# Attention with scores in 64-row tiles: the product with the remainder keys as two column tiles, and a rewritten table of steps

## The chip, the cores and the metric

The kernel runs on one core of one Trainium2 chip. The metric is the device time of one execution in microseconds (us), as the median of several runs. The engines of the core appear in the profile under short names: PE is the matrix engine (TensorE), PEld its weight loads, DVE the vector engine, ACT the scalar engine, POOL is GpSimd, and SP the engine whose queue issues most of the transfers (SPq).

## What is computed

Eight batches of eight heads of attention over 576 positions with head size 64, with an additive position bias, and after it a mixture of eight experts over the 4608 rows that attention gives.

```python
scores = scale * np.matmul(q, k.transpose(0, 1, 3, 2)) + bias
attn = np.exp(scores - scores.max(-1)); attn /= attn.sum(-1)
x = np.matmul(attn, v)                 # (8, 8, 576, 64), then rows of 512
...
e_idx = np.argmax(x @ w_gate + modality_bias[modality_id], axis=1)
for e in range(E):
    h = np.maximum(x[mask] @ w1[e], 0.0)
    out[mask] = gate_w[mask, None] * (h @ w2[e])
```

## The kernel before, in words

Three stages follow each other: the bias table (up to about 65 us), attention (to about 642 us) and the expert tiles (to the end). Attention works on pairs of heads: 8 batches times 4 pairs are 32 pairs, and the two heads of a pair lie on partitions 0 to 63 and 64 to 127.

576 positions are 512 and a remainder of 64. The 512 main positions are cut into four chunks of 128 queries, and the 64 remainder queries of both heads make a fifth chunk of 128 rows. For one pair and one chunk the score product (`scores`, L435) is twelve matmuls for chunks 0 to 3: each head contracts over its own 64 rows, so the two heads sit in two 64-row tiles of the array and go side by side. The fifth chunk is six matmuls over all 128 rows.

DVE reads the scores out of PSUM, adds the bias and takes the minimum (L449), ACT takes the exponential (L464), PE turns the result round in 128x128 blocks (`etrans`, L479 to L490), and DVE or ACT copy those out to `eT`, which holds the weights for the 512 main keys. POOL gathers the weights for the 64 remainder keys of both heads (`compact`, L469), PE turns these too (`rtrans`, L507), and ACT copies them to `rT`: 64 remainder keys of head 0 on partitions 0 to 63, those of head 1 below.

The product with the values (`av`) makes 576 query columns in two halves of 288. A half is eight matmuls with `eT` (L527), each with 128 rows of keys and 64 columns of one head. The two heads lie at columns 0 and 64 of the array (`tile_position=(0, 64 * h)`). To a half belongs one product with the remainder keys, `rem` (L521): `vrem` holds the remainder values of head 0 and 1 as a block diagonal with zeros beside, so one 128x128 matmul serves both heads. It opens half 0 and closes half 1. A matmul in f32 stands as two instructions in the trace (the transposes, and the score product with its f32r operands, stand as one).

The outer loop (`attention`) runs over n, the pair, and u = 0 to 4, the chunk. In step (n, u) it goes through the letters of `ORDER[u]`, and each engine gets its instructions in that order:

- `S` scores of chunk u, `f` and `e` exponentials of head 1 and head 0, `C` the remainder copy on POOL
- `t` and `T` transposes of the chunk that was scored two units earlier, heads 0 and 1 (for the fifth chunk, `T` is the small product L490)
- `R` the remainder transposes of pair n-1
- `a A b c` the value product of pair n-1: half 0 in two parts, half 1 in two parts
- `0 1 2` transposes of q, k and the remainder rows of pair n+1 (`prep`, L403 to L409). DVE copies them out as a high and a low part (L338 or L340, and L334)
- `L` and `V` issue loads of q and k for pair n+2, and of v for pair n+1; `q` and `k` are POOL's copies of q and k for pair n+2
- `X` and `B` take the next routing step of the batch finished before: `X` those with PE work (L779, L802, L850, L872), `B` those without

A digit after a letter puts the copies out of PSUM off by that many letters. Two banks of PSUM (`xps`) serve `R`, `0`, `1`, `2`, `X` and the value product in turn: whoever takes a bank waits for the copy out of the one that had it before. The last value products (pair 31) run in a step n = 32 without scores.

Of the kernel before, what the change touches and what calls it, by code (L numbers as in the profile page):

```python
# [22 lines left out]
S = 576  # L23
# [87 lines left out]
class Attn:  # L111
# [398 lines left out]
    def av(self, n, half, part):  # L510

        nc = self.nc
        if half == 0 and part == 0:
            self.xT[n] = self.xTb[n // NP % 2][:, n % NP, :]
        if part == 0:
            self.avps = self.xbank()
        v = self.vmain[n]
        sl = slice(HS * half, HS * half + HS)
        ps = self.avps[:, 0:HS]

        rem = lambda **kw: nc.tensor.matmul(ps, self.vrem[n % 2], self.rT[:, sl], skip_group_check=True, **kw)  # L521
        if half == 0 and part == 0:
            rem(start=True, stop=False)
        for k in (0, 1) if part == 0 else (2, 3):
            for h in range(2):
                o = slice(64 * h, 64 * h + 64)
                nc.tensor.matmul(  # L527
                    ps[o, :],
                    v[:, h, k, :],
                    self.eT[:, h, k, sl],  # L530
                    start=half == 1 and k == 0,
                    stop=half == 0 and k == 3,
                    tile_position=(0, 64 * h),
                    skip_group_check=True,
                )
        if part == 1:
            if half == 1:
                rem(start=False, stop=True)
            self.take(f"av{half}", self.xT[n][:, sl], ps)
            self.avps = None  # L540
            if half == 1:
                del self.vmain[n]

    def first_steps(self, route):
# [34 lines left out]


    ORDER = (
# [5 lines left out]
    )  # L587

    def attention(self):
# [889 lines left out]
```

## Time and profile before

| | |
|---|---|
| median of 3 runs | 1091.09 us (1089.97 to 1091.13) |
| the profiled execution | 1091.33 us, its span 1089.4 us |
| PE busy | 1066.4 us, 98% of the span |
| PEld, DVE, ACT, POOL busy | 842.9, 736.7, 678.8, 246.6 us |
| granted TensorE clock, mean | 0.999 |

The span reaches from the first to the last instruction; the profiled execution has 1.9 us around it. Busy is the time in which an engine had an instruction under way. Matmuls are pipelined and overlap in the record, so what a group of them costs PE is read from the start of the group to the start of the next one.

### The profile page before, as it was taken

What the parts mean: (1) busy time and instruction counts of PE and PEld (TensorE: products, weight loads), DVE (VectorE), ACT (ScalarE), POOL (GpSimd) and SP (SyncE); (2) the same over time, 40 slices, a digit from 0 to 9 for tenths busy, and PEclk for the clock granted to TensorE, in tenths of its full rate; (3) what the DMA queues carried; (4) which work ended last, traced back from release to release, by engine and by line L of the source; (5) the groups of instructions that cost most, each with busy time, mean ns of one, the idle gap of its engine ahead of it and who ended that gap; (6) DMA issues with size and microseconds to landing.
All of it is one profiled execution on the core that took longest, in us unless ns stands there. A gap on an engine that the chain in (4) does not pass through costs nothing.

```text
span 1089.4 us, 23080 instructions
## 1 busy us (share of the span) xinstructions
PE 1066.4 (98%) x8580; PEld 842.9 (77%) x8580; DVE 736.7 (68%) x1580; ACT 678.8 (62%) x1333; POOL 246.6 (23%) x521
## 2 busy tenths in 40 slices
PE   6989999999999999999999999999999999999997
PEld 3456777777777777777776779999999999898986
DVE  7987768677686776766868756587455665545544
ACT  6776766767667667676676765654455554444544
POOL 1012222414224224142242221331110001101110
PEclk9999999999999999999999999999999999999999
DMA  5983412212212122222221511112113621151500
GB/s 164 219 192 116 144 43 77 69 56 74 69 52 92 54 67 69 55 84 60 56 88 49 201 45 40 59 64 70 58 49 117 240 100 52 38 215 48 195 31 32
DMA packets 71960, 98.19 MB, mean 90 GB/s; under 512 B 23054, under 2 KB 47886, under 8 KB 71842
## 3 DMA queue, kind: packets, MB, share of 16 engines
q1 hardware_dynamic: 65826, 77.62, 24.0%
q0 software_dynamic: 5920, 19.03, 4.8%
q8 instruction: 69, 1.13, 0.4%
q14 instruction: 49, 0.40, 0.1%
q10 hardware_dynamic: 96, 0.00, 0.0%
HBM read 135.62 MB, written 23.90 MB: 146 GB/s over the span
## 4 chain that ended last, share of the span: by engine, by line
PE 90%; DVE 1%; issue 1%; ACT 1%; POOL 0%; POOLq 0%; DVEq 0%; ACTq 0%
PE p L1200 18%; PE p L1217 18%; PE sps L435 14%; PE xps L527 13%; PE eps L479 10%; PE xps L521 4%; PE xps L403 3%; PE xps L872 2%; PE xps L1180 2%; PE xps L507 1%; PE eps L485 1%; PE xps L779 1%; PE xps L409 1%; DVE Eb L449 1%; PE p L1399 1%
## 5 line engine op out<-in xcount | busy, mean ns | idle before, releaser
L464 ACT ACTIVATE Eb<-Eb,mn 128x576 f32<-128x576 f32 x288 | 221.1, 770 | 37.2 <-DVE mn L449 36.8
L449 DVE CUSTOM_DVE_ANT_0 Eb<-sps,NBm 128x576 f32<-128x576 f32 x256 | 183.7, 755 | 83.2 <-PE sps L435 70.3
L435 PE MATMUL sps<-QK 64*128 64x288 f32 (+1 forms) x1728 | 172.8, 311 | 3.1 <-DVE mn L449 2.0
L435 PEld LDWEIGHTS sps<-QK 64*128 64x128 f32 (+1 forms) x1728 | 133.4, 185 | 44.3 <-DVE QK L338 16.4
L1200 PE MATMUL p<-QK,w1hi 128*128 128x256 f32 x1136 | 160.9, 284 | 0.0
L1203 DVE SCALAR_TENSOR_TENSOR hl<-p,hh 128x512 fp32r<-128x512 f32 x72 | 49.7, 691 | 154.5 <-ACT hh L1202 154.5
L527 PE MATMUL xps<-eT,vraw 128*64 128x288 f32 x1024 | 151.8, 418 | 0.0
L1200 PEld LDWEIGHTS p<-QK,w1hi 128*128 128x128 f32 x1136 | 147.0, 192 | 2.9 <-issue 1.8
L479 PE MATMUL eps<-idf,Eb 128*128 128x128 f32 x1024 | 143.9, 276 | 0.0
L479 PEld LDWEIGHTS eps<-idf,Eb 128*128 128x128 f32 x1024 | 115.6, 141 | 12.7 <-issue 5.7
L336 ACT ACTIVATE eT<-eps 128x512 f32<-128x512 f32 x192 | 106.6, 590 | 28.8 <-PE eps L479 15.2
L1202 ACT ACTIVATE hh<-p 128x512 fp32r<-128x512 f32 x72 | 43.0, 598 | 116.6 <-PE p L1200 112.6
L1217 PE MATMUL p<-w2hi,hh 128*128 128x512 f32 x288 | 114.2, 396 | 0.0
L1217 PE MATMUL p<-w2hi,hl 128*128 128x512 f32 x288 | 112.5, 391 | 0.0
L1226 POOL DMA_INDIRECT out<-mo,idt x36 | 38.5, 1069 | 322.4 <-ACT QK L1183 222.2
L469 POOL COPY rem<-Eb 128x128 f32<-128x128 f32 x128 | 37.8, 296 | 301.8 <-ACT Eb L464 226.4
L527 PEld LDWEIGHTS xps<-eT,vraw 128*64 128x64 f32 x1024 | 62.2, 136 | 53.5 <-issue 25.4
L1163 DVE TENSOR_TENSOR w2lo<-NBm,w2hi 128x1024 fp32r<-128x1024 f32 x72 | 88.2, 1225 | 16.2 <-ACT w2hi L1162 16.1
L1200 PE MATMUL p<-QK,w1lo 128*128 128x256 f32 x568 | 91.3, 283 | 0.0
L1163 DVE TENSOR_TENSOR w1lo<-NBm,w1hi 128x1024 fp32r<-128x1024 f32 x72 | 84.2, 1231 | 0.2 <-ACT w1hi L1162 0.2
L1225 ACT ACTIVATE mo<-p,gates 128x512 f32<-128x512 f32 x36 | 24.8, 689 | 89.1 <-PE p L1217 74.4
L1200 PEld LDWEIGHTS p<-QK,w1lo 128*128 128x128 f32 x568 | 78.3, 192 | 0.0
(221 smaller groups left out, 1685.7 us busy)
## 6 DMA issues: line engine op xcount, KB each, us to landing
NBm<-moe_w SPq DMA_DIRECT2D x23, 2048.0 KB
NBm<-moe_w SPq DMA_DIRECT2D x44, 1024.0 KB
NBr<-xg SPq DMA_DIRECT2D x20, 516.0 KB
NBm<-xTb SPq DMA_DIRECT2D x32, 288.0 KB
qraw<-q SPq DMA_DIRECT2D x32, 256.0 KB
kraw<-k SPq DMA_DIRECT2D x32, 256.0 KB
vraw<-v SPq DMA_DIRECT2D x32, 256.0 KB
xg<-blank SPq DMA_DIRECT2D x9, 516.0 KB
```

Source lines behind the costliest of these rows:

```text
L336: self.nc.scalar.activation(out, ps, AF.Copy, scale=scale)
L435: nc.tensor.matmul(self.sps[h][:, half, 0:HS], QK[o, q, qs], QK[o, k, HS * half : HS * half + HS], start=i == 0, stop=i == 2, skip_group_c ...
L449: nc.vector.tensor_tensor_reduce(out=e.rearrange("p (t w) -> p t w", t=2), in0=self.sps[h][:, :, 0:HS], in1=nb.rearrange("p (t w) -> p t w ...
L464: self.nc.scalar.activation(e, e, AF.Exp, bias=mn, scale=-1.0, accum_out=sm)
L479: nc.tensor.transpose(ps[:, k, :], e[:, part, P * k : P * k + P], self.idf)
L521: rem = lambda **kw: nc.tensor.matmul(ps, self.vrem[n % 2], self.rT[:, sl], skip_group_check=True, **kw)
L527: nc.tensor.matmul(ps[o, :], v[:, h, k, :], self.eT[:, h, k, sl], start=half == 1 and k == 0, stop=half == 0 and k == 3, tile_position=(0, ...
L1163: self.nc.vector.tensor_tensor(l, w, h.bitcast(F32), op=ALU.subtract)
L1200: nc.tensor.matmul(ps[:, a, :], w[:, c, fs], x[:, c, :], start=i == 0, stop=i == len(ops) - 1)
L1202: nc.scalar.activation(hh[:, sl, :], ps, AF.Relu)
L1203: nc.vector.scalar_tensor_tensor(hl[:, sl, :], ps, 0.0, hh[:, sl, :].bitcast(F32), op0=ALU.max, op1=ALU.subtract)
L1217: nc.tensor.matmul(ps, h[:, f, sl], m[:, f, :], start=i == 0, stop=i == len(ops) - 1)
```

## The change

The remainder product becomes two matmuls of 64 columns, one for each head, at the same column positions as the products with `eT`. Each still contracts over all 128 rows of `rT` and takes 64 columns of `vrem`. The same edit rewrites `ORDER`.

```diff
-        rem = lambda **kw: nc.tensor.matmul(ps, self.vrem[n % 2], self.rT[:, sl], skip_group_check=True, **kw)
+        def rem(**kw):
+            for h in range(2):
+                o = slice(64 * h, 64 * h + 64)
+                nc.tensor.matmul(
+                    ps[o, :], self.vrem[n % 2][:, o], self.rT[:, sl], tile_position=(0, 64 * h), skip_group_check=True, **kw
+                )
+
...
     ORDER = (
-        "S X B t R1 T3 f e C L",
-        "01 t3 S a T 11 A f e C",
-        "S B t2 X e f k C q T2",
-        "b S e c B t1 T2 f V C",
-        "S B X 2 t T e B",
+        "L X S t R1 T3 f e C",
+        "0 t1 S f 11 e C a A2 B T",
+        "S B t3 e X f T3 C b",
+        "S c e k f t3 q T1 C",
+        "B S B X 22 t e V T1 B",
     )
```

What the table does to PE's instructions shows in unit u = 1 (here of a step in the middle of attention, from the last score matmul of chunk 1 to the first of chunk 2). The names are those of the code; xps_77 and xps_78 are the two PSUM banks. Before:

```order
L435 MATMUL sps_724<-QK_73 128x288
L521 MATMUL xps_77<-rT,vrem_110 128x288
L527 MATMUL xps_77<-eT,vraw_4133 64x288 x4
L490 MATMUL eps_726<-idf,Eb 64x64 x2
L403 MATMUL xps_78<-idf,qks_109 128x128 x4
L527 MATMUL xps_77<-eT,vraw_4133 64x288 x4
L435 MATMUL sps_723<-QK_73 128x288
```

and with the change (its lines are numbered 6 higher from `av` on):

```order
L435 MATMUL sps_724<-QK_73 128x288
L403 MATMUL xps_77<-idf,qks_109 128x128 x4
L524 MATMUL xps_78<-rT,vrem_110 64x288 x2
L533 MATMUL xps_78<-eT,vraw_4192 64x288 x8
L490 MATMUL eps_726<-idf,Eb 64x64 x2
L435 MATMUL sps_723<-QK_73 128x288
```

The transposes of k (L403) have moved ahead of the value product, whose two parts now stand in one piece behind the remainder product. The value product has moved to the other bank, xps_78, which the transposes of q used in the same unit.

On DVE the rows around the same place change in one step of four. The rows of before run from the second score read-out of chunk 0 (L449; its row without a source is the minimum that it leaves) to the first of chunk 1, in a step in which a routing step `B` (the one-hot rows, L827 to L837) falls on unit 0:

```order
L449 ISA Eb,mn_0_1_4619<-sps_724,NBm 128x576
L449 ISA mn_0_1_4619 128x1
L827 SCALAR_TENSOR_TENSOR oh<-lgs_4583,rev 128x40
L830 TENSOR_REDUCE mx_4601<-oh 128x5
L831 TENSOR_TENSOR oh<-oh,mx_4601 128x40
L832 TENSOR_TENSOR oh<-oh,valid 128x40
L837 TENSOR_TENSOR ohb<-ohb,oh 128x8 x5
L340 TENSOR_SCALAR QK_73<-xps_78 128x512
L334 SCALAR_TENSOR_TENSOR QK_73<-xps_78,QK_73 128x512
L449 ISA Eb,mn_1_0_4680<-sps_723,NBm 128x576
```

With the change:

```order
L449 ISA Eb,mn_0_1_4661<-sps_724,NBm 128x576
L449 ISA mn_0_1_4661 128x1
L340 TENSOR_SCALAR QK_73<-xps_78 128x512
L334 SCALAR_TENSOR_TENSOR QK_73<-xps_78,QK_73 128x512
L449 ISA Eb,mn_1_0_4704<-sps_723,NBm 128x576
L449 ISA mn_1_0_4704 128x1
L449 ISA Eb,mn_1_1_4706<-sps_724,NBm 128x576
L449 ISA mn_1_1_4706 128x1
L338 CAST QK_73<-xps_77 128x512
L334 SCALAR_TENSOR_TENSOR QK_73<-xps_77,QK_73 128x512
L833 SCALAR_TENSOR_TENSOR oh<-lgs_4613,rev 128x40
```

The nine one-hot instructions now come behind the copies of both q (L340, L334) and k (L338, L334). Elsewhere on DVE only small routing steps change places with a score read-out or a copy of `eT`. On PE the routing transposes of unit 0 (`X`) now come ahead of the scores of chunk 0, not behind them. On ACT the two copies of unit 1 that end half 0 (`rT`, 64 columns, and `xTb`) come behind the exponentials of chunk 1, and the copy that ends half 1 comes ahead of those of chunk 3. On SP the loads `L` move from the end of unit 0 to its start and `V` from unit 3 to unit 4; on POOL `k` and `q` move from unit 2 to unit 3.

## Rows read from the trace of the kernel before

**Rows 1.** The page: busy time of the engines; the group of the score read-outs

```profile
PE 1066.4 (98%) x8580; PEld 842.9 (77%) x8580; DVE 736.7 (68%) x1580; ACT 678.8 (62%) x1333; POOL 246.6 (23%) x521
...
L449 DVE CUSTOM_DVE_ANT_0 Eb<-sps,NBm 128x576 f32<-128x576 f32 x256 | 183.7, 755 | 83.2 <-PE sps L435 70.3
```

**Rows 2.** Busy time by stretch, attention's: us, each engine's busy, clock, DMA share

```profile
85.00:640.00 555.00, 552.37 (x4751) 404.97 (x4751) 399.65 (x1055) 387.20 (x924) 169.72 (x360) 1.00 0.26 79
```

**Rows 3.** What PE waited for from 85 to 640 us: total, times, longest

```profile
PE xps L507 <- DVE QK L1184: 1.6, 1, 1.6
PE sps L435 <- DVE QK L338: 0.5, 1, 0.5
```

**Rows 4.** Timeline of PE over unit 1 of a step: start, duration, instruction

```profile
312.23 0.60 PE L485 MATMUL eps<-idf,Eb 128*128 128x128 f32 x4
312.76 1.06 PE L435 MATMUL sps<-QK 64*128 64x288 f32 x12
313.75 0.75 PE L521 MATMUL xps<-rT,vrem 128*128 128x288 f32 x2
314.44 1.19 PE L527 MATMUL xps<-eT,vraw 128*64 128x288 f32 x8
315.46 0.28 PE L490 MATMUL eps<-idf,Eb 128*64 128x64 f32 x4
315.67 0.65 PE L403 MATMUL xps<-idf,qks 128*128 128x128 f32 x4
316.26 1.19 PE L527 MATMUL xps<-eT,vraw 128*64 128x288 f32 x8
317.38 0.80 PE L435 MATMUL sps<-QK 64*128 64x288 f32 x8
```

**Rows 5.** The same timeline, where half 1 ends in unit 3

```profile
305.14 0.75 PE L521 MATMUL xps<-rT,vrem 128*128 128x288 f32 x2
305.73 1.04 PE L479 MATMUL eps<-idf,Eb 128*128 128x128 f32 x8
```

**Rows 6.** Timeline of PE in the step without scores, n = 32

```profile
638.51 3.08 PE L527 MATMUL xps<-eT,vraw 128*64 128x288 f32 x24
641.52 0.75 PE L521 MATMUL xps<-rT,vrem 128*128 128x288 f32 x2
642.21 1.61 PE L779 MATMUL xps<-xTb,wgb 128*32 128x512 f32 x8
```

**Rows 7.** Timeline of PE: transposes behind a score group, and behind transposes

```profile
308.94 1.56 PE L435 MATMUL sps<-QK 64*128 64x288 f32 x12
310.43 0.66 PE L479 MATMUL eps<-idf,Eb 128*128 128x128 f32 x4
310.92 0.60 PE L507 MATMUL xps<-idf,rem 128*128 128x128 f32 x4
311.36 0.60 PE L479 MATMUL eps<-idf,Eb 128*128 128x128 f32 x4
```

**Rows 8.** Timeline of DVE, an ordinary step, and of PE behind it

```profile
349.21 0.69 DVE L334 SCALAR_TENSOR_TENSOR QK<-xps,QK 128x512 fp32r<-128x512 f32 x1
...
349.74 0.75 PE L521 MATMUL xps<-rT,vrem 128*128 128x288 f32 x2
```

**Rows 9.** Timeline of DVE in the step of rows 4, with one-hot

```profile
312.00 0.20 DVE L827 SCALAR_TENSOR_TENSOR oh<-lgs,rev 128x40 f32<-128x40 f32 x1
...
313.82 0.68 DVE L340 TENSOR_SCALAR QK<-xps 128x512 fp32r<-128x512 f32 x1
314.54 0.69 DVE L334 SCALAR_TENSOR_TENSOR QK<-xps,QK 128x512 fp32r<-128x512 f32 x1
```

**Rows 10.** What SP's queue waited for at the load of v

```profile
SPq L375 <- PE xps L527: 333.5, 30, 12.7
```

**Rows 11.** By line: weight loads in ns, least, median, most

```profile
L521 PEld LDWEIGHTS xps<-rT,vrem x128: 186/189/192, 83.0 to 641.6; 128*128 128x128 f32 x128
...
L527 PEld LDWEIGHTS xps<-eT,vraw x1024: 132/137/138, 83.7 to 640.9; 128*64 128x64 f32 x171
```

## The prediction

> **What bounds the kernel now.** I read the page's busy times first: PE is busy for 98% of the span, DVE for 68% and ACT for 62% [rows 1]. Then the stretch of attention alone: of 555 us PE is busy for 552, DVE for 400, ACT for 387, and the granted clock is 1.00 [rows 2], the higher of its two levels. PE's waits in this stretch come to about 2 us [rows 3]. So PE sets the pace here, and a busy PE is no proof that each of its slots is needed: matmuls overlap in the record. That is why I go on to the timeline and read slots, from the start of one group to the start of the next. They repeat to a few hundredths of a microsecond from step to step, so one step is enough.
>
> **What a slot is made of.** The clean measure is the long run of products with `eT` in the last step: 24 instructions from 638.51 to 641.52, 3.01 us [rows 6]. A group of eight takes 1.02 when the next group has the same column tiles (314.44 to 315.46) and 1.12 when it has not (316.26 to 317.38) [rows 4]; so leaving the tiling costs 0.10. (3.01 - 0.10) / 12 = 0.2425 us is what two instructions, one for each head, take side by side. Four of these are 0.97, so entering the tiling costs 1.02 - 0.97 = 0.05. Four transposes take 0.44 behind transposes (310.92 to 311.36) and 0.49 behind scores (310.43 to 310.92) [rows 7], and 0.53 when scores follow (312.23 to 312.76) [rows 4]: changing to or from them costs about 0.05 and 0.09 as well. The trace calls none of this waiting; it is time in which nothing new starts at a change of tile shape.
>
> The remainder product of before has a shape of its own among column tiles. In half 0 it holds PE from 313.75 to 314.44, 0.69 us [rows 4]; in half 1 from 305.14 to 305.73, 0.59 [rows 5]. As two column tiles it would be four instructions, two beside two: 2 x 0.2425 = 0.485. No row shows two column tiles that stream the same rows, so this has bounds: 0.485 if the two go side by side as the heads of L527 do, 0.97 if one goes after the other. I take 0.485, since form, row count and order of issue are those of L527.
>
> **Unit 1, half 0.** Before, from the end of the scores to the next scores: 0.69 remainder, 1.02 products, 0.21 the small product L490, 0.59 transposes of k, 1.12 products, in all 317.38 - 313.75 = 3.63 us [rows 4]. After: transposes of k between two other shapes, again 0.59; then remainder and all products in one piece, 0.05 + 10 x 0.2425 = 2.475; then L490, 0.21, which now pays for the change to scores in place of that to transposes. Sum 3.275. Saved: 0.355, of which 0.69 - 0.485 = 0.205 is the tiles, and 1.12 - 0.97 = 0.15 the order, since the products' second part is no longer entered and left on its own.
>
> **Unit 3, half 1.** The products before the remainder no longer leave their tiling; the remainder does it for them. The products' 1.12 [rows 4] and the remainder's 0.59 [rows 5] become 0.05 + 6 x 0.2425 + 0.10 = 1.605, 0.105 less. The eight transposes behind now pay 0.05 for a change that they did not have [rows 7]. Saved: 0.055.
>
> **The sum.** Steps n = 1 to 30 have both the value product and the transposes of k: 30 x (0.355 + 0.055) = 12.30 us. Step 31 has no transposes of k, so the tiles alone: 0.205 + 0.055 = 0.26. In step 32 transposes precede the first remainder product, which has their shape; it and the products take 0.485 + 0.10 + 1.02 before and 0.09 + 0.05 + 6 x 0.2425 after, 0.01 less, and the second falls from 0.69 [rows 6] to 0.485: together 0.215. In all 12.8 us. The profiled execution took 1091.33 us; less 12.8 that is 1078.5. The median of the runs lies 0.24 below the profiled one, so I forecast **1078.3 us**.
>
> **What else the order moves, and what covers it.** The value product now uses the bank that the transposes of q had, so the remainder product waits until DVE has copied q out. In an ordinary step DVE ends that at 349.21 + 0.69 = 349.90, and the remainder product stood at 349.74 [rows 8]; it now starts 0.59 later, at 350.33, so 0.43 us of cover is left. In the seven steps with one-hot the copy ended at 315.23 against 313.75 [rows 9]. Left there it would cost 1.48 - 0.59 = 0.89 each; but the order listing puts one-hot behind the copies, which then come 313.82 - 312.00 = 1.82 us earlier, so these steps are as the ordinary ones. What is queued behind one-hot now is the score read-out of chunk 2, and for that wait the scores of chunk 3. From the end of chunk 1's scores DVE has four read-outs of 0.755 [rows 1], two copies of 0.69 [rows 8] and one-hot, 6.2 us, before these. PE comes to them after 3.28 (above), 0.99 for the scores of chunk 2, and transposes, routing transposes, transposes and products, 0.49 + 0.44 + 0.53 + 1.12: 6.85. About 0.6 is left, less what DVE starts late.
>
> On ACT, the copies of `rT` and of half 0 now stand behind two exponentials instead of before them; the next use of their PSUM is in unit 2, about 2 us after half 0 ends, and ACT has 30% idle in this stretch [rows 2]. On POOL `k` and `q` come a unit later, and are read in unit 1 of the next step, two units on. On SP the load of v already stands waiting for PE, 333.5 us over 30 times [rows 10], about 11 us each: its buffer comes free only when the value product ends, so a unit later in the queue costs little, and its reader comes more than a step (17 us) later. `L` behind it moves half a unit earlier. `X` before the scores of chunk 0 has as many changes of shape as behind them. I cost all of these at nothing. One delay stays: in steps with a reduction of the logits on DVE, the scores of chunk 0 wait in their middle for the last copy of k, 1.49 in place of about 1.0 us [rows 7]; the order on DVE there is unchanged. It comes in about seven steps, 3.4 us in all.
>
> **Rivals.**
> *The two tiles don't overlap* (the other side). Both stream the same rows of `rT`, which L527's never do. If the second tile waits for the first, each of 64 remainder products costs 0.485 more: 31 us, and the time is 1078.3 + 31.0 = 1109.3, slower than before. It decides from 12.8 / 64 = 0.20 us on, 41% of the second tile. Against it: nothing in the rows hints that the moving rows' place matters. 3 in 100.
>
> *Weight loads come into the open.* A load of 64 columns takes 137 ns, one of 128 columns 189 [rows 11]. Four for two are 548 for 378 ns, 0.17 more; if loads were not hidden, 64 times, 10.9 us come back and 1089.2 is left, no change by measurement. Against it: eight loads of one group of L527 are 1.10 us, and the group takes 0.97 between entry and exit. 2 in 100. The Trainium skill, "TensorE: Matmul & The Clock Gate", section on packing small matmuls, says that a weight load overlaps running matmuls only when its row group differs; column tiles share all their rows, so by that rule this rival would hold. The trace of L527 disagrees, and I go by the trace.
>
> *A new wait eats the order's gain.* The cover of 0.43 us at the remainder product is gone if DVE is late in unit 0 by as much, or ACT holds a bank. Then the 30 x 0.15 = 4.5 us of the order come back: 1082.8. The routing steps moved within DVE speak for it, the 28% idle time of DVE against it. 8 in 100.
>
> *The delay at chunk 0's scores goes too*, because other work now precedes them: 3.4 us more, 1074.9. DVE's order speaks against it. 3 in 100.
>
> *The gain is given back behind attention*, because the expert tiles wait for transfers whose time doesn't shrink: up to all of it, 1091. DMA's share is 0.26 in attention [rows 2], so this is 2 in 100.
>
> **How the numbers follow.** The forecast has 82 in 100. Reading slots to 0.01 us leaves about 1.3 us over 62 products and 30 changes. The range runs from 1075.5, towards the case that gains more, to 1083.5, past the new wait: 90 in 100 lie in it. A measurement of this kernel tells 0.2%, 2.2 us, from no change. Faster hold the forecast, the new wait and the larger gain, 0.93; the same the loads and the giving back, 0.04; slower the tiles without overlap, 0.03.
>
> **What would show it.** Right: the slot of the remainder product in half 0 at about 0.49 us with no edge before the products; products with `eT` and remainder in unit 1 in one piece of about 2.5 us; 3.28 us between the scores of chunks 1 and 2; PE's waits in attention not above 3 us; the expert tiles the same length, begun 12 to 13 us earlier. Wrong: pairs of L524 that start 0.24 us apart instead of a few ns, or PE waiting at L524 for DVE's L334, or at the scores of chunk 3 for L449.

## The result and the profile after

| | before | after |
|---|---|---|
| median of 4 runs | 1091.11 us (1089.97 to 1091.89) | 1079.79 us (1079.48 to 1081.2) |
| the profiled execution | 1091.33 us | 1081.2 us |
| attention, from the first remainder transpose (L507) of step 1 to that of step 32 | 554.82 us | 543.59 us |

The ratio is 0.9896, with a 95% interval of 0.9884 to 0.9909: 11.3 us faster. The forecast was 1078.3 us, 12.8 less than before. Among the four runs of after the profiled one is the longest, by 1.3 to 1.7 us; its trace begins attention 1.4 us later than that of before (last section), and the other three have no trace.

The page after, part 1:

```profile
PE 1055.7 (98%) x8708; PEld 843.4 (78%) x8708; DVE 733.8 (68%) x1580; ACT 677.0 (63%) x1333; POOL 247.5 (23%) x521
```

PE has 128 instructions more than in [rows 1], two for each of 64 remainder products, and is busy 10.7 us less. The stretch of attention after by busy time (columns as in [rows 2]):

```profile
85.00:628.00 543.00, 540.23 (x4864) 404.47 (x4865) 397.93 (x1059) 385.15 (x923) 168.36 (x357) 1.00 0.27 80
```

PE is as full as in [rows 2] and still sets the pace.

What PE waited for after, from 85 to 628 us (total, times, longest), beside [rows 3]:

```profile
PE xps L507 <- DVE QK L1190: 1.6, 1, 1.6
PE sps L435 <- DVE QK L338: 0.7, 2, 0.5
```

The timeline of PE after, units 1 to 3 of one step, to set beside [rows 4, 5]:

```profile
327.88 0.66 PE L403 MATMUL xps<-idf,qks 128*128 128x128 f32 x4
328.46 0.71 PE L524 MATMUL xps<-rT,vrem 128*64 128x288 f32 x4
329.00 2.11 PE L533 MATMUL xps<-eT,vraw 128*64 128x288 f32 x16
330.94 0.28 PE L490 MATMUL eps<-idf,Eb 128*64 128x64 f32 x4
331.15 1.07 PE L435 MATMUL sps<-QK 64*128 64x288 f32 x12
...
335.72 1.19 PE L533 MATMUL xps<-eT,vraw 128*64 128x288 f32 x8
336.74 0.66 PE L524 MATMUL xps<-rT,vrem 128*64 128x288 f32 x4
337.33 1.09 PE L479 MATMUL eps<-idf,Eb 128*128 128x128 f32 x8
338.18 1.04 PE L435 MATMUL sps<-QK 128*128 128x288 f32 x6
```

Read the starts, not the durations. Transposes of k 0.58, remainder product 0.54, products 1.94, L490 0.21: 331.15 - 327.88 = 3.27 us in place of the 3.63 of [rows 4]. The four instructions of L524 stand as one row; within it the trace has two starts at 328.46 and 328.47 and two at 328.76, so the heads go in pairs. In unit 3 the remainder product holds 0.59 us as before (337.33 - 336.74), but the products ahead of it 1.02 in place of 1.12.

### The profile page after: what moved, and what is told of

Its sections match the earlier page's. It is cut to its first block, busy times and chain, and to the rows that moved or that the text cites. A ratio compares the mean times of both kernels' runs of the same rounds, so it can differ in the third digit from the quotient of the medians.

```text
span 1079.4 us, 23357 instructions
## 1 busy us (share of the span) xinstructions
PE 1055.7 (98%) x8708; PEld 843.4 (78%) x8708; DVE 733.8 (68%) x1580; ACT 677.0 (63%) x1333; POOL 247.5 (23%) x521
## 4 chain that ended last, share of the span: by engine, by line
PE 89%; DVE 2%; issue 1%; ACT 1%; POOL 0%; POOLq 0%; DVEq 0%; ACTq 0%
PE p L1206 19%; PE p L1223 18%; PE sps L435 14%; PE xps L533 12%; PE eps L479 11%; PE xps L524 3%; PE xps L403 3%; PE xps L878 2%; PE xps L1186 1%; PE xps L507 1%; PE eps L485 1%; PE xps L785 1%; DVE Eb L449 1%; PE xps L409 1%; PE p L1405 1%
## 5 line engine op out<-in xcount | busy, mean ns | idle before, releaser
L449 DVE CUSTOM_DVE_ANT_0 Eb<-sps,NBm 128x576 f32<-128x576 f32 x256 | 183.7, 755 | 100.9 <-PE sps L435 95.9
L479 PE MATMUL eps<-idf,Eb 128*128 128x128 f32 x1024 | 146.9, 278 | 0.0
L533 PE MATMUL xps<-eT,vraw 128*64 128x288 f32 x1024 | 143.4, 412 | 0.0
L479 PEld LDWEIGHTS eps<-idf,Eb 128*128 128x128 f32 x1024 | 112.4, 141 | 24.4 <-issue 18.0
L336 ACT ACTIVATE eT<-eps 128x512 f32<-128x512 f32 x192 | 109.5, 587 | 24.0 <-PE eps L479 19.2
L533 PEld LDWEIGHTS xps<-eT,vraw 128*64 128x64 f32 x1024 | 67.8, 136 | 48.6 <-issue 8.7
```

The source lines that it names most:

```text
L336: self.nc.scalar.activation(out, ps, AF.Copy, scale=scale)
L449: nc.vector.tensor_tensor_reduce(out=e.rearrange("p (t w) -> p t w", t=2), in0=self.sps[h][:, :, 0:HS], in1=nb.rearrange("p (t w) -> p t w ...
L479: nc.tensor.transpose(ps[:, k, :], e[:, part, P * k : P * k + P], self.idf)
L533: nc.tensor.matmul(ps[o, :], v[:, h, k, :], self.eT[:, h, k, sl], start=half == 1 and k == 0, stop=half == 0 and k == 3, tile_position=(0, ...
```

## The experiments

Each kernel was timed beside the kernel before, which stood at 1090.9 to 1091.0 us; "attention" is the span of the table above. Differences of less than about 2 us between two medians are read from attention, since the stretch ahead of it varies by over 1 us from execution to execution.

**Tiles alone, order alone.** `e1_tiles` is the kernel after with the old table, `e2_order` the kernel before with the new one.

Of each edit the lines of unit 0 and 1 are shown; the other three go the same way.

```diff
--- after
+++ e1_tiles
-        "L X S t R1 T3 f e C",
-        "0 t1 S f 11 e C a A2 B T",
+        "S X B t R1 T3 f e C L",
+        "01 t3 S a T 11 A f e C",
...
--- before
+++ e2_order
-        "S X B t R1 T3 f e C L",
-        "01 t3 S a T 11 A f e C",
+        "L X S t R1 T3 f e C",
+        "0 t1 S f 11 e C a A2 B T",
...
```

> The remainder product as two column tiles, in the order of steps of before. Theory (a slot is streaming plus a cost at each change of tile shape, about 0.05 on entering and 0.10 on leaving): half 0 saves 0.69 - 0.485 = 0.205 us a step, half 1 about 0.05, so 8 us in all: 1083 us, and PE goes from the scores of chunk 1 to those of chunk 2 in about 3.43 us. The rival that the two edits simply add, each with a share of its own, expects the same here; it parts from the theory in the run with the order alone.

> The new order of steps, the remainder product as one 128x128 matmul as before. Theory (cost at changes of shape): in the new order the remainder product stands behind the transposes of k, which have its shape, so it needs no change of its own there; unit 1 then takes about 0.49 + 0.59 + 2.0 + 0.21 = 3.28 us, the same as with both edits, and only half 1 keeps its 0.05. So the order alone gives nearly the whole gain: 30 x 0.35 = 10.5 us less 0.7 for a wait of the rank step, 1081.3 us. Rival (the edits add, as the prediction split them: 0.15 a step for the order): 4.5 less 0.7, 1087.3 us, and 3.48 us in unit 1.

Measured: e1 1083.71 us (ratio 0.9934, 0.9920 to 0.9947; attention 547.26), e2 1081.67 us (0.9915, 0.9901 to 0.9928; attention 545.64). Alone the parts bring 7.2 and 9.2 us, which adds to 16.4; together they bring 11.3. The timeline of PE in unit 1 shows why. In e1:

```profile
312.47 0.71 PE L524 MATMUL xps<-rT,vrem 128*64 128x288 f32 x4
...
315.90 1.06 PE L435 MATMUL sps<-QK 64*128 64x288 f32 x12
```

In this order stand scores, remainder, products, L490, transposes, products, and scores again: 315.90 - 312.47 = 3.43, so tiles alone save 0.20 of the 3.63. The same timeline in e2:

```profile
310.64 0.65 PE L403 MATMUL xps<-idf,qks 128*128 128x128 f32 x4
311.13 0.65 PE L521 MATMUL xps<-rT,vrem 128*128 128x288 f32 x2
311.71 2.16 PE L527 MATMUL xps<-eT,vraw 128*64 128x288 f32 x16
...
313.92 1.07 PE L435 MATMUL sps<-QK 64*128 64x288 f32 x12
```

This takes 313.92 - 310.64 = 3.28, as with both parts. The old remainder product now stands behind the transposes of k, which have its shape, so one edge is gone without tiles. A remainder product costs 0.49 plus its edges in either form (last section). With the new order the tiles earn in unit 3, where no transposes precede the product: 1.5 of the 2.05 us between e2 and after. In unit 1 they bring nothing in an ordinary step.

**The step with the ranks.** In after, routing step `X` of unit 2 (the rank products, L856 and L857) waited for DVE's last one-hot instruction. `e3_rank_later` puts `X` behind the second transposes.

```diff
-        "S B t3 e X f T3 C b",
+        "S B t3 e f T3 X C b",
```

> The changed kernel with the routing step X of unit 2 behind the transposes of the second head instead of between the two. Theory (the rank matmul of eight steps waits about 0.09 us for the one-hot rows, which DVE now computes later): the first rank matmul's slot falls from 0.11 to 0.03 us, 0.7 us in all, 1079.1 us, which the time alone can hardly tell. Rival (the 0.11 is the cost of that matmul at this place, without a wait): the slot stays at 0.11 and the time at 1079.8.

Measured: 1078.42 us (0.9888, 0.9873 to 0.9904), attention 542.52. The timelines of PE and DVE in one such step before:

```profile
174.82 0.19 PE L850 MATMUL xps<-ohb,tri 128*128 128x48 bf16 x1
174.85 0.18 PE L851 MATMUL xps<-ohb,ones 128*128 128x48 bf16 x1
...
168.89 0.97 DVE L837 TENSOR_TENSOR ohb<-ohb,oh 128x8 bf16<-128x8 bf16 x5
```

The same after:

```profile
173.99 0.19 PE L856 MATMUL xps<-ohb,tri 128*128 128x48 bf16 x1
174.10 0.18 PE L857 MATMUL xps<-ohb,ones 128*128 128x48 bf16 x1
...
173.09 0.97 DVE L843 TENSOR_TENSOR ohb<-ohb,oh 128x8 bf16<-128x8 bf16 x5
```

The timeline of PE in e3:

```profile
172.70 0.19 PE L856 MATMUL xps<-ohb,tri 128*128 128x48 bf16 x1
172.73 0.18 PE L857 MATMUL xps<-ohb,ones 128*128 128x48 bf16 x1
```

Before, the one-hot rows were ready about 5 us early. After, DVE ends them at 173.09 + 0.97 = 174.06 and L857 starts 0.04 later, 0.11 after L856 in place of 0.03. In e3 the gap is 0.03 again. The wait is too short for the list of waits. Attention falls by 1.07 us, 0.9 of it in seven steps at 0.13 each, of which 0.08 to 0.09 is the wait; the rest goes with the four transposes that no longer stand behind the short rank products.

**Does issue order make the tiles overlap?** `e5_heads_apart` issues four products of head 0 and then four of head 1. `e11_heads_far` issues all ten instructions of half 0 for head 0, then the ten for head 1.

```diff
--- after
+++ e5_heads_apart
-        for k in (0, 1) if part == 0 else (2, 3):
-            for h in range(2):
+        for h in range(2):
+            for k in (0, 1) if part == 0 else (2, 3):
--- after
+++ e11_heads_far
-        def rem(**kw):
-            for h in range(2):
+        def rem(hs=(0, 1), **kw):
+            for h in hs:
...
-        if half == 0 and part == 0:
-            rem(start=True, stop=False)
-        for k in (0, 1) if part == 0 else (2, 3):
-            for h in range(2):
+        if half == 0:
+            rem((part,), start=True, stop=False)
+        for k in (0, 1, 2, 3) if half == 0 else (0, 1) if part == 0 else (2, 3):
+            for h in (part,) if half == 0 else (0, 1):
```

> The changed kernel with the products with eT issued head by head: in each part the two of head 0 and then the two of head 1, instead of the heads in turn; the remainder product stays a neighbouring pair. Theory (two column tiles go side by side only where they are neighbours in the order of issue, since matmuls start in that order): a part of eight instructions is no longer 4 x 0.2425 us but nearly one after the other with an overlap at the change of head, about 1.45 to 1.9 us instead of 0.97; with four parts in 32 steps that is 60 to 125 us more, 1140 to 1205 us. Rival (a tile that is free takes its next matmul whatever stands before it in the queue): no change, 1080 us.

> The changed kernel with half 0 issued head by head over its whole length: remainder and four products with eT of head 0, ten instructions, and then the ten of head 1. The run with the heads apart by four instructions kept the two column tiles side by side. If a tile takes its next matmul however far back it stands in the queue: no change, about 1080 us, and 2.48 us from the first L524 to L490. If PE looks ahead only some instructions: part of the ten go alone, and half 0 takes up to 4.85 us, 76 us more in all.

One execution each: e5 1082.28 us, attention 545.19; e11 1127.54 us, attention 589.77. The timeline of PE in half 0 of a step, in e5:

```profile
311.58 2.16 PE L533 MATMUL xps<-eT,vraw 128*64 128x288 f32 x16
313.52 0.34 PE L490 MATMUL eps<-idf,Eb 128*64 128x64 f32 x4
```

Sixteen products still take 1.94 us: the theory that heads must alternate in issue order fell. What attention takes longer, 1.6 us, is some 0.05 a step: head 1 starts about 0.06 us after head 0, and L490 holds 0.27 in place of 0.21. The same timeline in e11:

```profile
309.89 0.70 PE L524 MATMUL xps<-rT,vrem 128*64 128x288 f32 x2
310.43 1.38 PE L533 MATMUL xps<-eT,vraw 128*64 128x288 f32 x5
311.40 0.46 PE L524 MATMUL xps<-rT,vrem 128*64 128x288 f32 x1
311.64 0.41 PE L533 MATMUL xps<-eT,vraw 128*64 128x288 f32 x1
...
312.92 0.33 PE L490 MATMUL eps<-idf,Eb 128*64 128x64 f32 x2
313.15 0.89 PE L533 MATMUL xps<-eT,vraw 128*64 128x288 f32 x3
313.88 0.28 PE L490 MATMUL eps<-idf,Eb 128*64 128x64 f32 x2
```

Here seven instructions of head 0 start, 0.24 us apart, before the first of head 1 does at 311.40, and three of head 0 are still to come. From the remainder product to the last L490 it is 3.99 us in place of 2.48, so a step takes 1.5 us more. PE does start the free tile's instruction ahead of older ones of the other tile, but only across a few. At 311.40 three older ones were left, and at 311.16, with four left, nothing of head 1 started. In e5 the first of head 1 also passes three, and in e11 L490 starts at 312.92 ahead of the three L533 from 313.15 on. So three is what these two traces show; other distances were not run.

**Half 1 in one piece.** If entering and leaving the tiling costs 0.15, joining the two parts of half 1 in unit 3 might save it once more.

```diff
-        "S B t3 e X f T3 C b",
-        "S c e k f t3 q T1 C",
+        "S B t3 e X f T3 C",
+        "S b c e k f t3 q T1 C",
```

> The changed kernel with the two parts of half 1 joined behind the scores of chunk 3 (b moves from the end of unit 2 to behind S of unit 3), which takes away one more entry and exit of the column tiles. If PE's slots alone decide: 0.15 us a step less, 4.7 us, 1075 us. Theory (PE work between two score products also covers DVE's read-out of the first, 2 x 0.755 us and its late start): between the scores of chunks 2 and 3 only 1.0 to 1.5 us of PE work are left where 2.6 were, so PE waits for the read-out 0.3 to 1.2 us in each step; slower than the changed kernel by 5 to 30 us, 1085 to 1110 us.

Measured: 1091.51 us (1.0003, 0.9993 to 1.0012), attention 555.60, 12.0 more than after. The timeline of PE at the scores of chunk 3:

```profile
319.26 0.40 PE L435 MATMUL sps<-QK 64*128 64x288 f32 x1
319.94 1.05 PE L435 MATMUL sps<-QK 64*128 64x288 f32 x11 [0.28 <-DVE mn L449]
320.92 2.16 PE L533 MATMUL xps<-eT,vraw 128*64 128x288 f32 x16
```

And the largest of its waits:

```profile
PE sps L435 <- DVE mn L449: 4.8, 17, 0.3
```

The scores of chunk 3 hold PE for 1.66 us here and 0.99 after, because the products that stood ahead of them were the time in which DVE read the scores of chunk 2 out of their banks. Of these 0.67 us the list of waits has 0.28 in this step, and 4.8 in all steps; only the starts show the whole. Over 31 steps 12.0 us are 0.39 each, net of what the joined tiling saves.

**The same price elsewhere.** The transpose of the remainder rows of k (L408) is the only one with 64 rows; it and its neighbours hold slots of 0.16 to 0.20 us, where a 128-row transpose among its like takes 0.11. The timeline of PE after:

```profile
339.59 0.27 PE L408 MATMUL xps<-idf,krem 64*128 64x64 f32 x1
339.79 0.33 PE L409 MATMUL xps<-idf,qrem 128*128 128x128 f32 x1
339.96 1.04 PE L479 MATMUL eps<-idf,Eb 128*128 128x128 f32 x8
```

`e4_krem_full` makes it a 128-row transpose, with 64 rows of zeros beneath.

```diff
+        self.kremb = [cp.tile([P, 2, D], F32, name=f"kremb{k}") for k in range(2)]
...
+        rem = self.kremb[n % 2][0:64]
...
-            nc.tensor.transpose(ps[:, 0:64], self.krem.pop(n).rearrange("p h d -> p (h d)"), self.idf[0:64, 0:64])
+            nc.tensor.transpose(ps[:, 0:128], self.krem.pop(n).rearrange("p h d -> p (h d)"), self.idf)
```

> The changed kernel with the remainder rows of k in a tile of 128 rows, the lower 64 of them loaded and the others zero, so that their transpose (L408, 64 rows of contraction) is a full 128x128 one like those before and behind it. Theory (a change of shape costs PE a fixed time wherever it stands): the two slots of 0.20 us around it and the slow start behind it fall to 0.11 each, about 0.24 us a step, 31 times: 7.5 us less than the changed kernel, 1072.3 us. Rival (the 0.20 is the wait for the transfers and copies of these operands, not the shape): no change, 1079.8 us.

Measured: 1074.88 us (0.9856, 0.9841 to 0.9871), attention 539.03. Ordinary steps take 16.24 in place of 16.48, the 0.24 expected. But the steps with the reduction of the logits, in which the scores of chunk 0 already waited 0.5 us, gain nothing. The timelines of PE and DVE in such a step of e4:

```profile
160.80 0.66 PE L436 MATMUL sps<-QK 64*128 64x288 f32 x6
161.83 0.79 PE L436 MATMUL sps<-QK 64*128 64x288 f32 x6 [0.37 <-DVE QK L339]
162.55 0.66 PE L480 MATMUL eps<-idf,Eb 128*128 128x128 f32 x4
...
160.74 0.77 DVE L818 TENSOR_REDUCE lgs<-lw 128x40 f32<-128x320 f32 x1
161.43 0.34 DVE L339 CAST QK<-xps 128x192 fp32r<-128x192 f32 x1
```

PE arrives earlier, but the copy of the remainder keys still stands behind the reduction on DVE: the slot grows from 1.49 to 1.75. Two ways to take that delay away were run. `e7_keys_first` puts PE's remainder transposes ahead of `X` in unit 4; `e8_all` joins e3, e4 and e7.

```diff
-        "B S B X 22 t e V T1 B",
+        "B S B 2 X t e V T1 B",
```

> The changed kernel with the remainder transposes (op 2) of unit 4 ahead of the routing step X and their copies not put off. Theory (the delay inside the scores of chunk 0, 1.49 for 1.0 us, comes from DVE, which does the logits' reduction before it copies the remainder keys): the copies now come first, the delay goes, about 0.49 us in eight steps, 3.9 us less than the changed kernel: 1076 us, and those slots fall to 1.0. Rival (the scores wait for another reason, such as ACT or the transfer): unchanged, 1079.8 us.

> The changed kernel with all three: X of unit 2 later, the remainder rows of k as a full 128x128 transpose, and the remainder keys' copies ahead of X in unit 4. Theory: the full transposes gave 0.24 us a step but lost it in the eight steps whose scores waited for DVE; with that wait gone they give it in all 31. From the run with the later rank step (1078.4 us) 7.5 and 3.9 less: 1067 us. Rival (DVE then is late somewhere else in those steps, so that PE's time comes back as another wait): 1071 to 1075 us.

Measured: e7 1080.62 us (0.9893, 0.9877 to 0.9910; attention 543.74), e8 1077.29 us (0.9869, 0.9853 to 0.9886; attention 540.14). In e7 the delayed steps fall from 17.51 to 17.03, but the step behind each rises from 17.53 to 17.80 and the one ahead of it from 17.72 to 17.86, so that next to nothing is left. The waits of e8 name where it went:

```profile
PE xps L879 <- DVE QK L335: 2.1, 7, 0.3
```

`X` (L879 there) now takes a PSUM bank that a copy of `prep` still holds. In e7 the list has no such wait, but the same steps, those behind the delayed ones, grew by 0.27. The lost time moved, and e8, meant to add up to 1067 us, comes out above even its rival's 1071 to 1075 and by attention 1.1 us slower than e4 alone. `e9_reduce_later` leaves PE alone and moves DVE's reduction of the logits behind the copies, to the next routing step; `e10_all2` joins e3, e4 and e9.

```diff
-                if part == 1:
-                    lg = rt.tile(C5, F32, tag="lg", name=f"lgs{b}")
-                    nc.vector.tensor_reduce(lg, t.rearrange("p c h e -> p c e h"), axis=AX.X, op=ALU.add)
-                    st["lg"] = lg
...
         def s_top():
-            lg = st["lg"]
+            lg = st["lg"] = rt.tile(C5, F32, tag="lg", name=f"lgs{b}")
+            nc.vector.tensor_reduce(lg, st["t"].rearrange("p c h e -> p c e h"), axis=AX.X, op=ALU.add)
```

> The changed kernel with the reduction of the logits (0.75 us on DVE) moved from the routing step X of unit 4 into the step B at the end of that unit, so that DVE copies the remainder keys before it. Nothing moves on PE. Theory (the delay of 0.49 us in the scores of chunk 0 is DVE's order, and moving X itself only shifted a wait to the bank that the next X takes): the slots of 1.49 fall to 1.0 in eight steps and no other slot grows: 3.9 us less, 1075.9 us. Rival (whatever is moved there, DVE's lateness comes back in another slot): 1078 to 1080 us.

> The changed kernel with the rank step later, the full transposes of the remainder keys and the reduction later. Theory: the saving of the full transposes is kept in all 31 steps once the scores no longer wait for DVE: attention 1.1 + 7.5 + 3.9 = 12.5 us shorter than with the change alone, 1067.3 us. Rival: some of it comes back as a wait of PE for DVE, 1069 to 1073 us, and then PE's waits for DVE in the trace name the place.

Measured: e9 1077.10 us (0.9877, 0.9862 to 0.9892), attention 539.73; e10 1069.66 us (0.9802, 0.9788 to 0.9815), attention 533.01. The timelines of DVE and PE in a step of e9 that was delayed before:

```profile
163.21 0.36 DVE L334 SCALAR_TENSOR_TENSOR QK<-xps,QK 128x192 fp32r<-128x192 f32 x1
163.48 0.78 DVE L820 TENSOR_REDUCE lgs<-lw 128x40 f32<-128x320 f32 x1
...
163.12 1.07 PE L435 MATMUL sps<-QK 64*128 64x288 f32 x12
164.12 0.66 PE L479 MATMUL eps<-idf,Eb 128*128 128x128 f32 x4
```

The copies come first, the scores' slot is 1.00 in place of 1.49, and no other step grows. Five of the seven steps fall from 17.51 to 17.03; the first and the last, which waited longer, fall by 0.63 and 0.79. e10 is the fastest kernel here, 10.1 us under the change. That it stays above 1067.3 us is in part due to the steps ahead of the formerly delayed ones, which fall only from 17.72 to 17.61 where ordinary ones fall by 0.24; this was not followed up.

## Why the prediction was right, and where its sum was off

**What bounds the kernel, and what a slot is made of: shown.** PE's pace is set by matmul time plus changes of tile shape, which PE's list of waits does not name. e1, e2 and after come out at 3.43, 3.28 and 3.27 us in unit 1 with the same matmul work; e4 took 0.24 a step from another place by the same reading.

**The tiles go side by side: shown.** The slot of 0.54 holds an entry of 0.05 and 0.49; foretold was 0.485. Had the tiles followed each other, it would be about 1.0. Of the reason given, "form, row count and order of issue", the order of issue is not needed in its strict sense (e5), but must be near (e11).

**Weight loads stay hidden, but for the first of a shape: shown.** Loads of L524 take 137 ns each, four 548, and the slot is 0.54 with the streaming alone at 0.49; the rival's 0.17 more did not come. The entry of 0.05, which the prediction had as a price without a cause, is a load that is not hidden (last section).

**Unit 1: 0.355 foretold, 0.344 measured on average.** The split into 0.205 for the tiles and 0.15 for the order was only one way to share it out: the order alone brings nearly all of it (e2). The sum was right because both parts were costed together, edge by edge; the two parts measured alone add to 16.4 us.

**Unit 3: 0.055 foretold, 0.048 measured.**

**"I cost all of these at nothing": this step failed, in one place.** I asked who waits behind one-hot on DVE and found the score read-outs. The reader of the one-hot rows themselves, the rank product of unit 2, I left out. It lost 0.09 us in seven steps, 0.6 us. The rest of that step held. At the remainder product the bank was free in time, by the timeline of DVE after, in the step shown above:

```profile
327.36 0.69 DVE L334 SCALAR_TENSOR_TENSOR QK<-xps,QK 128x512 fp32r<-128x512 f32 x1
```

It ends at 328.05, and L524 starts at 328.46: 0.41 of cover, 0.43 foretold. The delay in the scores of chunk 0 stayed at 1.49, as foretold, save in the first of the delayed steps, where DVE starts a copy 0.17 us late without a wait that the profile shows, and the scores hold PE for 1.63 (164.28 to 165.91). Its price of 3.4 us was right to half a microsecond: e9 got back 3.9. Nothing was given back behind attention: the expert tiles begin 10.0 us earlier in the profiled execution (633.72 against 643.75), and 11.4 with the 1.4 us that it had lost ahead of attention.

**The rivals.** The tiles overlap, the loads add nothing new, nothing comes back later, and the delay stays. The new wait is the one that came in part: not at the remainder product, where the rival had it for 4.5 us, but at the ranks, at 0.6.

**The account.** Of 12.56 us foretold between the two remainder transposes of the table, 11.23 came: 0.33 less in unit 1, 0.2 in units 3 and 4, 0.7 in unit 2 (0.6 of it the ranks), 0.13 where `X` moved ahead of the scores. Apart from the ranks these are a hundredth of a microsecond a step, the reading of slots, and a few single steps, among them 0.15 in the first of the delayed ones.

## What to carry to other kernels

When the bound engine is full and waits for nothing, read the starts of its groups: a change of tile shape cost 0.05 to 0.10 us to enter and 0.10 to leave here, and neighbours of one shape, by order or by padding, save it. Cost such changes on the whole sequence, since two edits may remove the same edge, and ask for each moved instruction not only what stands behind it on its engine but who reads what it writes. Work between two groups also covers the engine that empties their banks (e6), and a delay taken from one consumer of a bank may turn up at the next (e7); moving the late engine's own work out of the way (e9) did not.

## What the runs showed of the hardware that was not expected

**Start order.** In e11 the remainder matmul of head 1 started at 311.40, while three matmuls of head 0 that were issued earlier started later, from 311.64 on. The Trainium skill, "TensorE: Matmul & The Clock Gate", Part 3 on packing small matmuls, says that matmuls start and end strictly in program order; the trace differs for column tiles, over three instructions.

**Edges belong to pairs of shapes.** The remainder product needs the same 0.49 us with 128 columns or as two column tiles side by side; the neighbours decide what it holds (before: 0.69 between scores and column tiles; e2: 0.58 between transposes of its own shape and column tiles; after: 0.54, ahead of column tiles like itself). The old product's 0.69 is thus 0.49 with an entry and an exit of 0.10 each, of which e2 saves the first and unit 3 [rows 5] the second. So two edits that remove the same edge do not add. What the entry is stands in the weight loads (PEld), first in after, then in e2:

```profile
328.46 0.20 PEld L524 LDWEIGHTS xps<-rT,vrem 128*64 128x64 f32 x4 [0.17 <-issue]
328.76 0.39 PEld L533 LDWEIGHTS xps<-eT,vraw 128*64 128x64 f32 x4
...
311.03 0.30 PEld L521 LDWEIGHTS xps<-rT,vrem 128*128 128x128 f32 x2
```

Within one shape a load runs ahead: that of L533 begins at 328.76, its product at 329.00; in e2, behind transposes of the same shape, that of L521 begins at 311.03 and its product at 311.13. Where the shape changes it does not: the first loads of L524 begin at 328.46, with their products. The first matmul of such a group lasts longer, and the next follows later by as much (328.76, then 329.00). Durations in ns, least, median, most, before and after:

```profile
L521 PE MATMUL xps<-rT,vrem x128: 406/407/511, 83.0 to 641.9; 128*128 128x288 f32 x128
L524 PE MATMUL xps<-rT,vrem x256: 406/406/458, 85.0 to 631.8; 128*64 128x288 f32 x128
```

So entering costs 0.10 us where a load takes 189 ns (L521) and 0.05 where it takes 137 (L524, as L527 in [rows 11]). What the 0.10 on leaving is, no run here shows.

**The clock ahead of attention.** Busy time and clock after from 60 to 65 us (columns as in [rows 2]):

```profile
60.00:65.00 5.00, 3.53 (x29) 1.52 (x32) 3.58 (x12) 2.19 (x5) 0.00 (x0) 0.67 0.67 182
```

In the profiled execution of after, PE waited 2.3 us for DVE at the end of the bias table (L198 for L939), in code that the change does not touch, and the granted clock was 0.67 on average from 60 to 65 us, part of it at the lower level of 1.2 GHz. Before, the same wait was 1.3 us, and the clock stayed at 1.00. Profiled executions of e1, e2, e5 and e7 show such a fall too, with waits of 2.1 to 2.2 us; e8 and e11 waited 2.1 to 2.2 us and kept 1.00. Step 1 begins 1.4 us later in the profile of after than in that of before (81.59 against 80.20). Most of this goes with the clock: in e8 PE's wait ended at the same 61.47 us as in after, the clock stayed at 1.00, and step 1 began at 80.35.
